# Attention with routed experts on one core: float index tables from GpSimd, three one-row products, and a later first value load

## The chip, the cores and the metric

The kernel runs on one core of a Trainium2 chip. The metric is the device time of one execution in microseconds (us); lower is better. Engines are named as in the profile: PE is TensorE (PEld its weight loads), DVE is VectorE, ACT is ScalarE, POOL is GpSimd, SP is SyncE, which here only issues transfers.

## The reference

Attention over q, k, v of shape (4, 8, 768, 64) with four sink positions and a sliding window of 128, then a two-level mixture of experts over the 3072 tokens of 512 features: a group (of 4) and an expert in it (of 4) are picked by argmax, each expert is a two-layer network (512 to 1024 to 512), and its output is scaled by the product of the two gate probabilities.

```python
scores = scale * np.matmul(q, k.transpose(0, 1, 3, 2))
keep = (pos[None, :] < n_sink) | ((rel >= 0) & (rel < window))
a = softmax(np.where(keep, scores, -1e9))          # rel = query position - key position
x = (a @ v)                                        # as 3072 tokens x 512
g = argmax(x @ w_group); e = argmax(x @ w_expert[g])
out = gate(g) * gate(e) * (relu(x @ w1[g, e]) @ w2[g, e])
```

`n_sink` and `window` are 64-bit inputs, handed over as four 32-bit words.

## The kernel before, in words

One function, `moe_attention`, builds the whole program. The attention goes over 24 tiles of 128 queries (6 tiles in each of 4 batches) in a loop that is written as a pipeline (line 1214): in iteration i the scores of tile i, the transposes and first value products of earlier tiles, the logits of tile i-3 and pieces of the routing are issued. Each engine runs its instructions in the order of the program text (`Pinned`, line 125, keeps that order), so the text of the loop body is the schedule. Behind the loop stand the expert layers, which read 128 weight blocks and scatter their outputs.

A tile's scores are written into two halves of PSUM (four heads each). `maxima(i, g)` (line 770) adds the mask on VectorE and takes the negative maximum, one instruction per head; on tiles that do not begin a batch a predicated copy comes first. `exps(i, g)` (line 782) runs one exponential per head on ScalarE. `trans`, `evac`, `sink_t`, `sink_evac`, `sink_rows` and `sink_pack` transpose the probabilities and bring them to SBUF (ScalarE copies, GpSimd selections); `values` multiplies them with the values; `norm` and `norm_logits` scale the result and add the routing logits on VectorE.

What the change touches is the opening, lines 184 to 312, and three later places:

- Lines 184 to 187: two integer tables by GpSimd iota, `dif` (row minus column) and `coli` (column).
- Lines 268 to 278: VectorE casts both to float (`diff`, `col`), copies the two diagonal 64x64 blocks into `dq`, and makes `isu` (where `dq` is negative) and `rel`.
- Lines 279 to 283: the four words are cast (`nf1`); PE runs `warm(WARM)`, 14 filler matmuls on zeros, then one product of a row of ones with the words, which spreads them to all 128 partitions, then `warm(WARM2)`, six more fillers.
- Lines 286 to 305: the masks of the first tile of a batch (`msk[:, 0]`) and a part of the later ones. The words of each number are put together here: the low word, plus 2**32 where it is negative, plus 2**32 times the high word (`lneg`, `sv`).
- Lines 309 to 314: `other_masks`, called in iteration 0 after the tile's maxima, makes the masks of the other tiles.
- Lines 335 to 344: `tables`, called in iteration 3 after `sink_pack(3)`, makes the constants of the routing, `trib` from `diff` among them.
- Lines 1211 and 1212: the loads of the first sink values (`load_s(0)`, 128 KB) and of tile 0's values (`load_v(0)`, 512 KB), ahead of the loop. All loads but a part of tile 0's keys go through SP's queue. `load_q(i + 2)` and `load_k(i + 2)` stand in the loop; the queries have two buffers, so tile 2's wait for tile 0's scores.

The function `warm(k, dst)` (line 200) issues k filler matmuls. `FILL` gives further fillers in iterations 0 to 2 (8, 10 and 6).

Of the kernel before, what the change touches and what calls it, by code (L numbers as in the profile page):

```python
# [10 lines left out]
F32 = mybir.dt.float32  # L11
F32R = mybir.dt.float32r
BF16 = mybir.dt.bfloat16
I32 = mybir.dt.int32
U32 = mybir.dt.uint32
AF = mybir.ActivationFunctionType
ALU = mybir.AluOpType
# [5 lines left out]
P = 128  # L23
B, H, S, D = 4, 8, 768, 64
# [21 lines left out]
NEG = -1.0e30  # L46
# [55 lines left out]
FIRST = 21  # L102
TAIL = (8, 8)
PW = G + NE
WARM = 14
WARM2 = 6
FILL = [8, 10, 6]


# [38 lines left out]
def moe_attention(tc, kqT, vN, vS, nsw, wgx, wgd, w1, w2, out):  # L148
    nc = Pinned(tc)
    v = nc.vector  # L150
    with ExitStack() as top, ExitStack() as att:
# [5 lines left out]
        gp = fl.enter_context(tc.tile_pool(name="gp", bufs=6, side="left"))  # L157
# [9 lines left out]
        ob = [ps_a.tile([P, DM], F32, name=n) for n in ("lg", "po")]  # L167

        def const(shape, dt, name):
            return cp.tile(shape, dt, name=name)  # L170
# [3 lines left out]
        ni = const([1, 4], I32, "ni")  # L174
        nc.sync.dma_start(ni, nsw)
        colm = const([P, P], F32, "colm")
# [4 lines left out]
        qb = wk.tile([P, NQ, HP, P], F32, name="qb", bufs=1)  # L181
        xx = un[:, 0:NDC * W].rearrange("p (c w) -> p c w", w=W)
        hx = un[:, NDC * W:(NDC + NFC) * W].rearrange("p (f w) -> p f w", w=W)
        dif = gp.tile([P, P], I32, name="xg")
        nc.gpsimd.iota(dif, pattern=[[-1, P]], base=0, channel_multiplier=1)
        coli = gp.tile([P, P], I32, name="xg")
        nc.gpsimd.iota(coli, pattern=[[1, P]], base=0, channel_multiplier=0)
        act = const([P, 1], F32, "act")
        nc.gpsimd.memset(act, 0.0)
        nc.gpsimd.memset(colm[0:1], 1.0)  # L190
        nc.gpsimd.memset(kb[:, :, 0:BW], 0.0)
        vts, env, bat = {}, {}, {}

# [3 lines left out]
        def pair():  # L197
            return ps_p.tile([P, 2, 4 * P], F32, name="tp")

        def warm(k, dst=None):  # L200
            dst = pair()[:, 0, 0:192] if k and dst is None else dst
            for _ in range(k):
                nc.tensor.matmul(dst, wz[:, 0:P], wz, start=True, stop=True)
# [17 lines left out]
        def load_q(i):  # L221
            b, t = divmod(i, NT)
            nc.sync.dma_start(qb[:, i % NQ], kqT[b, t, :, KB:].rearrange("d (h q) -> d h q", h=HP))
# [7 lines left out]
        def room_v(i):  # L231
            vts[i] = wk.tile([P, 2, DM], F32, name="vv", bufs=3)

        def load_v(i):
            room_v(i)
            b, t = divmod(i, NT)
            nc.sync.dma_start(vts[i].rearrange("p f n -> p (f n)"), vN[b, t])

        def load_s(i):
            nc.sync.dma_start(vts[i - 1][SK].rearrange("p f n -> p (f n)"), vS[i // NT])  # L240
# [24 lines left out]

        route_reset(tab)

        diff = const([P, P], F32, "diff")
        v.tensor_copy(diff, dif)
        col = const([P, P], F32, "col")  # L270
        v.tensor_copy(col, coli)
        dq = gp.tile([P, D], F32, name="xg")
        for r in (0, D):
            v.tensor_copy(dq[r:r + D], diff[r:r + D, r:r + D])
        isu = gp.tile([P, D], F32, name="xg")
        v.tensor_scalar(isu, dq, 0.0, None, ALU.is_lt)
        rel = gp.tile([P, D], F32, name="xg")
        v.scalar_tensor_tensor(rel, isu, float(P), dq, ALU.mult, ALU.add)
        nf1 = const([1, 4], F32, "nf1")
        v.tensor_copy(nf1, ni)  # L280
        warm(WARM)
        nc.tensor.matmul(ob[0][:, 0:4], colm[0:1], nf1, start=True, stop=True)
        warm(WARM2)
        msk = const([P, 3, SW], F32, "msk")
        mb, ms, mc = msk[:, :, 0:D], msk[:, :, D:D + 2 * NSK], msk[:, :, D + 2 * NSK:]
        v.tensor_scalar(mb[0:D, 0], dq[0:D], 0.0, NEG, ALU.mult, ALU.add)
        v.tensor_scalar(ms[:, 0, 0:NSK], col[:, 0:NSK], 0.0, NEG, ALU.is_ge, ALU.mult)
        wd = const([P, 1], F32, "wd")
        nf = const([P, 4], F32, "nf")
        v.tensor_copy(nf, ob[0][:, 0:4])  # L290
        lneg = const([P, 2], F32, "lneg")
        v.tensor_scalar(lneg, nf[:, 0::2], 0.0, 4294967296.0, ALU.is_lt, ALU.mult)
        v.tensor_tensor(lneg, lneg, nf[:, 0::2], ALU.add)
        sv = const([P, 2], F32, "sv")
        v.scalar_tensor_tensor(sv, nf[:, 1::2], 4294967296.0, lneg, ALU.mult, ALU.add)
        nsk, win = sv[:, 0:1], sv[:, 1:2]
        v.tensor_scalar(wd, win, -float(D), None, ALU.add)
        snk = gp.tile([P, D], F32, name="xg")
        v.tensor_scalar(mc[:, 2], rel, win, NEG, ALU.is_ge, ALU.mult)
        v.tensor_scalar(snk, col[:, 0:D], nsk, NEG, ALU.is_lt, ALU.mult)  # L300
        v.tensor_scalar(mb[:, 2], dq, wd, NEG, ALU.is_ge, ALU.mult)
        v.scalar_tensor_tensor(mc[:, 0], isu, NEG, mc[:, 2], ALU.mult, ALU.add)
        v.tensor_tensor(mb[D:P, 0], mb[D:P, 2], snk[D:P], ALU.add)
        v.tensor_scalar(ms[:, 0, NSK:], col[:, 0:NSK], nsk, NEG, ALU.is_ge, ALU.mult)
        v.tensor_tensor(mc[0:D, 0], mc[0:D, 0], snk[0:D], ALU.add)
        selu = const([P, D], I32, "selu")
        val = const([P, NI], F32, "val")

        def other_masks():
            v.tensor_scalar(selu, dq, 0.0, None, ALU.is_lt)  # L310
            v.tensor_copy(ms[:, 2], ms[:, 0])
            v.tensor_copy(msk[:, 1], msk[:, 2])
            v.tensor_tensor(snk[0:D], snk[0:D], isu[0:D], ALU.mult)
            v.tensor_tensor(mc[0:D, 1], mc[0:D, 1], snk[0:D], ALU.add)
# [19 lines left out]

        def tables():
            v.tensor_scalar(colm, col, -float(P), None, ALU.add)
            v.tensor_scalar(trib, diff, 0.0, None, ALU.is_lt)
            v.tensor_scalar(rev, col[:, 0:4], -1.0, 4.0, ALU.mult, ALU.add)
            v.tensor_scalar(edge, col[:, 0:MAXT + 1], float(P), None, ALU.mult)
            v.tensor_copy(val, prti)  # L340
            v.tensor_scalar(gen[:, 0:1], win, 1.0, None, ALU.is_lt)
            v.tensor_scalar(gen[:, 1:2], win, float(P), None, ALU.is_gt)
            v.tensor_scalar(gen[:, 2:3], nsk, float(NSK), None, ALU.is_gt)
            v.tensor_reduce(gen[:, 3:4], gen[:, 0:3], AX.X, ALU.max)
# [136 lines left out]
        start = const([P, NE], F32, "start")  # L481
# [177 lines left out]
        xg, cg, later = {}, {}, []  # L659
# [548 lines left out]

        ew = early_work(PARTS[0][0])
        room_v(-1)  # L1210
        load_s(0)
        load_v(0)
        rest = None
        for i in range(NI):
            a, b, c = i - 1, i - 2, i - 3
            mid, far, old = a >= 0, b >= 0, c >= 0
            state["clk"] += 3.0
            scores(i, 0)
            scores(i, 1)
            if i + DEPTH < NI:  # L1220
                load_q(i + DEPTH)
            if mid:
                env["tp"] = pair()
                trans(a)
                evac(a, 0)
                evac(a, 1)
            warm(FILL[i] if i < len(FILL) else 0, ob[0][:, 224:416])
            if far:
                values(b, 0)
                load_s(b + 1)  # L1230
            if i + DEPTH < NI:
                load_k(i + DEPTH)
            if i == 0:
                load_v(1)
            if old:
                logits(c)
            if mid:
                sink_t(a)
            if old:
                natural(c)  # L1240
            maxima(i, 0)
            exps(i, 0)
            maxima(i, 1)
            if i == NI - 1:
                sink_evac(a)
            if old:
                norm(c)
            routing(1, ("pe",))
            exps(i, 1, (0, 1))
            if mid and i < NI - 1:  # L1250
                sink_evac(a)
            exps(i, 1, (2, 3))
            if mid:
                sink_rows(a)
            if i < NI - 1:
                sink_pack(i)
            if old:
                norm_logits(c)
            if i == 0:
                late_consts()  # L1260
            if i == 3:
                tables()
            state["clk"] += 3.0
            if far:
                values(b, 1)
                load_v(i)
                out_evac(b)
            if rest:
                rest()
                rest = None  # L1270
            put_gates(3)
            if later and not gates:
                gather(*later.pop(0))
            routing(UNITS.get(i, REND), (None, "rd"))
            if i and i % 2 == 0:
                sums(i - 1)
            rest = half.pop()() if half else wjob() if i < NI - 1 else None
            if i in HOOK:
                prefetch(min(RAW, len(raws) + 1))
# [372 lines left out]
```

## Time and profile before

| what | value |
|---|---|
| median of 3 runs | 489.07 us (487.38 to 489.42) |
| time of the profiled execution | 484.39 us |
| span of the profiled execution | 482.7 us |
| PE busy | 465.3 us (96%) |
| VectorE busy | 374.7 us (78%) |
| ScalarE busy | 330.2 us (68%) |
| GpSimd busy | 168.4 us (35%) |
| chain that ended last, by engine | PE 67%, DVE 17%, ACT 7%, issue 4%, POOL 3%, DMA 1% |

Times in the views are microseconds from the start of the span. A busy time counts instructions in flight; in a chain of waits each piece is followed by the work that it released. In a timeline a number in brackets is the idle time of the engine before the row, and behind the arrow what ended it.

### The profile page before, as it was taken

Reading aid. Unit: us, or ns where it says so; the run is one execution under the profiler, and the core shown is the slowest. Engines: PE = TensorE matmul, PEld = TensorE weight load, DVE = VectorE, ACT = ScalarE, POOL = GpSimd, SP = SyncE. Lnnn points to the kernel's source line nnn. Section 1 sums busy time; section 2 is a strip of 40 time slices with the busy share of each in tenths; the row PEclk is TensorE's granted clock in tenths of the full one; section 3 lists DMA queues with packets and bytes.
Section 4 is the critical chain, followed back from the end, with each engine's and each line's share of the span. In section 5 each row is a group of like instructions: output and inputs, shape, how many; then the busy total and the mean of one; then the engine's idle time right before and its main releaser. Section 6 shows DMA issues by size and latency. Waiting matters only on the chain.

```text
span 482.7 us, 14712 instructions
## 1 busy us (share of the span) xinstructions
PE 465.3 (96%) x5429; PEld 390.0 (81%) x5429; DVE 374.7 (78%) x1181; ACT 330.2 (68%) x858; POOL 168.4 (35%) x267
## 2 busy tenths in 40 slices
PE   7999999999989999999999999999999999999994
PEld 6788878888779888887989789569876977977974
DVE  7576888899989989987714876488687997999750
ACT  5999989899893445766615765278446786788741
POOL 3674765664662122221203124033302713103102
PEclk9999999999999999999999999999999999999998
DMA  8698878989978937934952358596949983999300
GB/s 260 177 286 277 275 250 245 272 258 318 289 233 274 336 103 245 311 135 150 377 217 85 110 176 299 197 330 267 311 169 372 411 314 111 362 405 337 108 22 30
DMA packets 58836, 117.09 MB, mean 243 GB/s; under 512 B 8574, under 2 KB 20990, under 8 KB 58754
## 3 DMA queue, kind: packets, MB, share of 16 engines
q1 hardware_dynamic: 54162, 102.65, 62.5%
q0 software_dynamic: 4320, 13.26, 7.8%
q8 instruction: 45, 0.74, 0.6%
q14 instruction: 37, 0.30, 0.2%
q10 hardware_dynamic: 272, 0.15, 0.1%
HBM read 103.25 MB, written 13.03 MB: 241 GB/s over the span
## 4 chain that ended last, share of the span: by engine, by line
PE 67%; DVE 17%; ACT 7%; issue 4%; POOL 3%; DMA 1%; POOLq 0%; DVEq 0%; SPq 0%; ACTq 0%
PE ph L118 30%; PE po L118 28%; PE tp L118 5%; ACT pt L118 3%; DVE sm L118 3%; DVE wlo L118 3%; PE ps L118 3%; DVE xt L118 2%; POOL pu L118 2%; ACT whi L118 1%; PE lg L118 1%; DVE ps L118 1%; ACT pa L118 1%; DVE lt L118 1%; DVE un L118 1%
## 5 line engine op out<-in xcount | busy, mean ns | idle before, releaser
L118 DVE TENSOR_TENSOR wlo<-rw,whi 128x1024 fp32r<-128x1024 f32 x112 | 135.0, 1223 | 24.9 <-ACT whi L118 23.5
L118 PE MATMUL ph<-un,whi 128*128 128x256 f32 (+9 forms) x576 | 128.0, 312 | 0.3
L118 PE MATMUL po<-whi,un 128*128 128x512 f32 (+5 forms) x384 | 127.8, 396 | 0.0
L118 ACT CAST whi<-rw 128x1024 fp32r<-128x1024 f32 (+1 forms) x115 | 115.6, 1025 | 10.5 <-DMA rw<-in_w 5.6
L118 POOL DMA_INDIRECT out<-ot,sidx x32 | 43.2, 1351 | 227.7 <-ACT ot L118 129.3
L118 PE MATMUL ph<-un,wlo 128*128 128x256 f32 (+10 forms) x416 | 99.1, 263 | 0.0
L118 PEld LDWEIGHTS ph<-un,whi 128*128 128x128 f32 x576 | 93.7, 189 | 2.2 <-DVE un L118 0.8
L118 PEld LDWEIGHTS po<-whi,un 128*128 128x128 f32 (+4 forms) x384 | 70.4, 185 | 25.1 <-issue 6.7
L118 ACT ACTIVATE pt<-sm,st 128x136 f32<-128x136 f32 x192 | 76.1, 402 | 7.4 <-DVE st L118 5.3
L118 PE MATMUL po<-wlo,un 128*128 128x512 f32 (+6 forms) x200 | 77.5, 389 | 0.0
L118 PEld LDWEIGHTS ph<-un,wlo 128*128 128x128 f32 x416 | 76.7, 189 | 0.6
L118 DVE CUSTOM_DVE_ANT_0 sm<-ps,msk 128x136 f32<-128x136 f32 x192 | 45.8, 296 | 7.3 <-PE ps L118 1.1
L118 PEld LDWEIGHTS po<-wlo,un 128*128 128x128 f32 (+5 forms) x200 | 36.0, 180 | 7.6
L118 POOL DMA_INDIRECT xg<-xd,gidx x30 | 33.1, 1104 | 24.2 <-DMA rw<-in_w 11.6
L118 PE MATMUL ps<-kb,qb 64*64 64x208 f32 (+1 forms) x768 | 38.4, 333 | 2.0 <-DVE st L118 1.4
L118 DVE TENSOR_TENSOR hc<-ph,hc 128x160 f32<-128x160 f32 (+6 forms) x64 | 21.3, 338 | 21.6 <-ACT hc L118 21.4
L118 POOL COPY pu<-spT 32x512 f32<-32x512 f32 x46 | 28.6, 649 | 26.3 <-ACT spT L118 25.4
L118 ACT ACTIVATION_READ_ACCUMULATOR pt<-sm,st 128x1 f32 x192 | 36.8, 192 | 0.0
L118 ACT ACTIVATE ot<-po,cg 128x512 f32<-128x512 f32 (+6 forms) x25 | 17.0, 681 | 28.1 <-PE po L118 28.1
L118 PEld LDWEIGHTS ps<-kb,qb 64*64 64x64 f32 x768 | 26.5, 132 | 7.3 <-DVE st L118 2.1
L118 POOL TENSOR_SCALAR_AFFINE_SELECT pu<-pa 64x512 f32<-64x512 f32 x40 | 26.4, 660 | 15.7 <-ACT pa L118 15.7
L118 ACT COPY hc<-ph 128x160 f32<-128x160 f32 (+6 forms) x64 | 19.4, 304 | 17.8 <-PE ph L118 17.0
(204 smaller groups left out, 717.6 us busy)
## 6 DMA issues: line engine op xcount, KB each, us to landing
rw<-in_w SPq DMA_DIRECT2D x128, 512.0 KB, 5.9
vv<-in_vN SPq DMA_DIRECT2D x24, 512.0 KB, 5.2
kb<-in_kqT SPq DMA_DIRECT2D x23, 288.0 KB, 3.9
qb<-in_kqT SPq DMA_DIRECT2D x24, 256.0 KB, 4.6
xd<-xt SPq DMA_DIRECT2D x24, 256.0 KB, 3.7
vv<-in_vS SPq DMA_DIRECT2D x24, 128.0 KB, 3.5
out<-ot,sidx POOLq DMA_INDIRECT x32, 4.9
xg<-xd,gidx POOLq DMA_INDIRECT x30, 4.9
```

The source lines that it names most:

```text
L118: r = f(*a, **k)
```

## The change

GpSimd writes the index tables as float: the two diagonal blocks straight into `dq`, and `col`; the casts and copies on VectorE are gone, and so is the full table `diff` in the opening. `tables()` makes `diff` when it needs it, by an iota of its own. The scalars' sign is taken from the cast words on one partition, and three products (low words by 1, sign flags by 2**32, high words by 2**32) add up in PSUM, with one filler behind each; VectorE copies the sum once. The mask of tile 0 is made from a table `relx` in which the upper part is already far away, and from `far`, which is `dq` plus 64. The table and the mask of the later tiles (`rel`, `mc[:, 2]`) move into `other_masks()`. The fillers go from 14 and 6 to 11 and 1. The two first value loads move into iteration 0, behind `load_k(2)`.

```diff
--- before.py
+++ after.py
@@ -102,8 +102,8 @@
 FIRST = 21
 TAIL = (8, 8)
 PW = G + NE
-WARM = 14
-WARM2 = 6
+WARM = 11
+WARM2 = 1
 FILL = [8, 10, 6]
 
 
@@ -181,13 +181,21 @@
         qb = wk.tile([P, NQ, HP, P], F32, name="qb", bufs=1)
         xx = un[:, 0:NDC * W].rearrange("p (c w) -> p c w", w=W)
         hx = un[:, NDC * W:(NDC + NFC) * W].rearrange("p (f w) -> p f w", w=W)
-        dif = gp.tile([P, P], I32, name="xg")
-        nc.gpsimd.iota(dif, pattern=[[-1, P]], base=0, channel_multiplier=1)
-        coli = gp.tile([P, P], I32, name="xg")
-        nc.gpsimd.iota(coli, pattern=[[1, P]], base=0, channel_multiplier=0)
+        mk = gp.tile([P, 6, D], F32, name="xg")
+        dq, far, isu, rel, relx, snk = (mk[:, k] for k in range(6))
+        col = const([P, P], F32, "col")
+
+        def count(out, **k):
+            nc.gpsimd.iota(out, base=0, allow_small_or_imprecise_dtypes=True, **k)
+
+        for r in (0, D):
+            count(dq[r:r + D], pattern=[[-1, D]], channel_multiplier=1)
+        count(col, pattern=[[1, P]], channel_multiplier=0)
         act = const([P, 1], F32, "act")
         nc.gpsimd.memset(act, 0.0)
         nc.gpsimd.memset(colm[0:1], 1.0)
+        two32 = gp.tile([1, P], F32, name="xg")
+        nc.gpsimd.memset(two32, 4294967296.0)
         nc.gpsimd.memset(kb[:, :, 0:BW], 0.0)
         vts, env, bat = {}, {}, {}
 
@@ -265,48 +273,35 @@
 
         route_reset(tab)
 
-        diff = const([P, P], F32, "diff")
-        v.tensor_copy(diff, dif)
-        col = const([P, P], F32, "col")
-        v.tensor_copy(col, coli)
-        dq = gp.tile([P, D], F32, name="xg")
-        for r in (0, D):
-            v.tensor_copy(dq[r:r + D], diff[r:r + D, r:r + D])
-        isu = gp.tile([P, D], F32, name="xg")
         v.tensor_scalar(isu, dq, 0.0, None, ALU.is_lt)
-        rel = gp.tile([P, D], F32, name="xg")
-        v.scalar_tensor_tensor(rel, isu, float(P), dq, ALU.mult, ALU.add)
-        nf1 = const([1, 4], F32, "nf1")
-        v.tensor_copy(nf1, ni)
+        v.scalar_tensor_tensor(relx, isu, -NEG, dq, ALU.mult, ALU.add)
+        v.tensor_scalar(far, dq, float(D), None, ALU.add)
+        nf1 = const([1, 6], F32, "nf1")
+        v.tensor_copy(nf1[:, 0:4], ni)
+        v.tensor_scalar(nf1[:, 4:6], nf1[:, 0:4:2], 0.0, None, ALU.is_lt)
         warm(WARM)
-        nc.tensor.matmul(ob[0][:, 0:4], colm[0:1], nf1, start=True, stop=True)
-        warm(WARM2)
+        for k, (w, x) in enumerate(((colm[0:1], nf1[:, 0:4:2]), (two32, nf1[:, 4:6]), (two32, nf1[:, 1:4:2]))):
+            nc.tensor.matmul(ob[0][:, 0:2], w, x, start=k == 0, stop=k == 2)
+            warm(WARM2)
         msk = const([P, 3, SW], F32, "msk")
         mb, ms, mc = msk[:, :, 0:D], msk[:, :, D:D + 2 * NSK], msk[:, :, D + 2 * NSK:]
         v.tensor_scalar(mb[0:D, 0], dq[0:D], 0.0, NEG, ALU.mult, ALU.add)
         v.tensor_scalar(ms[:, 0, 0:NSK], col[:, 0:NSK], 0.0, NEG, ALU.is_ge, ALU.mult)
-        wd = const([P, 1], F32, "wd")
-        nf = const([P, 4], F32, "nf")
-        v.tensor_copy(nf, ob[0][:, 0:4])
-        lneg = const([P, 2], F32, "lneg")
-        v.tensor_scalar(lneg, nf[:, 0::2], 0.0, 4294967296.0, ALU.is_lt, ALU.mult)
-        v.tensor_tensor(lneg, lneg, nf[:, 0::2], ALU.add)
         sv = const([P, 2], F32, "sv")
-        v.scalar_tensor_tensor(sv, nf[:, 1::2], 4294967296.0, lneg, ALU.mult, ALU.add)
+        v.tensor_copy(sv, ob[0][:, 0:2])
         nsk, win = sv[:, 0:1], sv[:, 1:2]
-        v.tensor_scalar(wd, win, -float(D), None, ALU.add)
-        snk = gp.tile([P, D], F32, name="xg")
-        v.tensor_scalar(mc[:, 2], rel, win, NEG, ALU.is_ge, ALU.mult)
         v.tensor_scalar(snk, col[:, 0:D], nsk, NEG, ALU.is_lt, ALU.mult)
-        v.tensor_scalar(mb[:, 2], dq, wd, NEG, ALU.is_ge, ALU.mult)
-        v.scalar_tensor_tensor(mc[:, 0], isu, NEG, mc[:, 2], ALU.mult, ALU.add)
-        v.tensor_tensor(mb[D:P, 0], mb[D:P, 2], snk[D:P], ALU.add)
+        v.tensor_scalar(mc[:, 0], relx, win, NEG, ALU.is_ge, ALU.mult)
+        v.tensor_scalar(mb[:, 2], far, win, NEG, ALU.is_ge, ALU.mult)
         v.tensor_scalar(ms[:, 0, NSK:], col[:, 0:NSK], nsk, NEG, ALU.is_ge, ALU.mult)
         v.tensor_tensor(mc[0:D, 0], mc[0:D, 0], snk[0:D], ALU.add)
+        v.tensor_tensor(mb[D:P, 0], mb[D:P, 2], snk[D:P], ALU.add)
         selu = const([P, D], I32, "selu")
         val = const([P, NI], F32, "val")
 
         def other_masks():
+            v.scalar_tensor_tensor(rel, isu, float(P), dq, ALU.mult, ALU.add)
+            v.tensor_scalar(mc[:, 2], rel, win, NEG, ALU.is_ge, ALU.mult)
             v.tensor_scalar(selu, dq, 0.0, None, ALU.is_lt)
             v.tensor_copy(ms[:, 2], ms[:, 0])
             v.tensor_copy(msk[:, 1], msk[:, 2])
@@ -334,6 +329,8 @@
 
         def tables():
             v.tensor_scalar(colm, col, -float(P), None, ALU.add)
+            diff = gp.tile([P, P], F32, name="xg")
+            count(diff, pattern=[[-1, P]], channel_multiplier=1)
             v.tensor_scalar(trib, diff, 0.0, None, ALU.is_lt)
             v.tensor_scalar(rev, col[:, 0:4], -1.0, 4.0, ALU.mult, ALU.add)
             v.tensor_scalar(edge, col[:, 0:MAXT + 1], float(P), None, ALU.mult)
@@ -1208,8 +1205,6 @@
 
         ew = early_work(PARTS[0][0])
         room_v(-1)
-        load_s(0)
-        load_v(0)
         rest = None
         for i in range(NI):
             a, b, c = i - 1, i - 2, i - 3
@@ -1231,6 +1226,8 @@
             if i + DEPTH < NI:
                 load_k(i + DEPTH)
             if i == 0:
+                load_s(0)
+                load_v(0)
                 load_v(1)
             if old:
                 logits(c)
```

## Rows read from the trace of the kernel before

**Rows 1.** Chain of waits in the opening: start us, us, what.
```profile
1.13 2.42 PE tp L118 x14
```
**Rows 2.** Timeline, ScalarE: first exponentials of tiles 0 and 4 (start us, us, instruction, idle before).
```profile
6.79 0.41 ACT L118 ACTIVATE pt<-sm,st 128x136 f32<-128x136 f32 x1 [4.01 <-DVE st L118]
...
27.06 0.42 ACT L118 ACTIVATE pt<-sm,st 128x136 f32<-128x136 f32 x1
```
**Rows 3.** Busy time in two stretches: us, PE, PEld, DVE, ACT, POOL, PEclk, DMA share, GB/s.
```profile
24.00:48.00 24.00, 23.45 (x622) 20.29 (x616) 17.86 (x100) 22.94 (x88) 14.54 (x28) 1.00 0.89 281
...
200.00:300.00 100.00, 100.00 (x627) 86.83 (x626) 66.65 (x142) 59.47 (x115) 22.19 (x21) 1.00 0.57 203
```
**Rows 4.** Timeline, PE, from the product to the fillers behind tile 0's scores.
```profile
3.48 0.59 PE L118 MATMUL lg<-nf,colm 1*128 1x4 f32 x2
4.00 0.87 PE L118 MATMUL tp<-wz 128*128 128x192 bf16 x6
4.81 1.16 PE L118 MATMUL ps<-kb,qb 64*64 64x136 f32 x32
5.90 0.83 PE L118 MATMUL lg<-wz 128*128 128x192 bf16 x8
```
**Rows 5.** Timeline, VectorE, from its first instruction to tile 0's first maximum.
```profile
1.38 0.84 DVE L118 CAST diff<-xg 128x128 f32<-128x128 int32 x1 [1.38 <-POOL xg L118]
...
3.17 0.15 DVE L118 CAST nf<-ni 1x4 f32<-1x4 int32 x1
...
4.11 0.16 DVE L118 COPY nf<-lg 128x4 f32<-128x4 f32 x1 [0.62 <-PE lg L118]
4.30 0.17 DVE L118 TENSOR_SCALAR lneg<-nf 128x2 f32<-128x2 f32 x1
...
5.13 0.25 DVE L118 TENSOR_SCALAR xg<-col,sv 128x64 f32<-128x64 f32 x1
5.29 0.25 DVE L118 TENSOR_SCALAR msk<-xg,wd 128x64 f32<-128x64 f32 x1
...
5.70 0.22 DVE L118 TENSOR_TENSOR msk<-msk,xg 64x64 f32<-64x64 f32 x1
5.94 0.23 DVE L118 TENSOR_SCALAR msk<-col,sv 128x4 f32<-128x4 f32 x1
6.08 0.21 DVE L118 TENSOR_TENSOR msk<-msk,xg 64x64 f32<-64x64 f32 x1
6.45 0.30 DVE L118 CUSTOM_DVE_ANT_0 sm<-ps,msk 128x136 f32<-128x136 f32 x1 [0.16 <-DVE msk L118]
```
**Rows 6.** Timeline, GpSimd: the two iotas.
```profile
1.12 0.42 POOL L118 IOTA xg<- 128x128 int32 x2
```
**Rows 7.** Transfers between 1.7 and 1.8, SP's queue: packets, MB, share.
```profile
q1 hardware_dynamic: 2, 0.00, 1.0%
```
**Rows 8.** Timeline, SP's queue and PE: a value load, tile 1's scores, tile 0's values.
```profile
6.88 0.50 SPq L118 DMA_DIRECT2D vv<-in_vN  x1
...
8.08 1.64 PE L118 MATMUL ps<-kb,qb 64*64 64x208 f32 x32 [1.35 <-DVE st L118]
...
15.88 1.15 PE L118 MATMUL po<-pa,vv 128*64 128x64 f32 x32
```
**Rows 9.** Page, transfers by kind: count, KB each, us from issue to landing.
```profile
vv<-in_vN SPq DMA_DIRECT2D x24, 512.0 KB, 5.2
```
**Rows 10.** Timeline, GpSimd: sink copies of tiles 0 and 3.
```profile
10.09 0.21 POOL L118 COPY sp<-pt 128x32 f32<-128x32 f32 x1 [6.95 <-ACT pt L118]
...
10.24 0.19 POOL L118 MEMSET sacc<- 128x16 f32 x3
...
25.55 0.21 POOL L118 COPY sp<-pt 128x32 f32<-128x32 f32 x1
```
**Rows 11.** Timeline, VectorE: the routing table and tile 4's first maximum.
```profile
23.91 0.21 DVE L118 TENSOR_SCALAR trib<-diff 128x128 bf16<-128x128 f32 x1
...
25.35 0.30 DVE L118 CUSTOM_DVE_ANT_0 sm<-ps,msk 128x136 f32<-128x136 f32 x1
```

## The prediction

> **What bounds the kernel now.** I read the page first (96% of the span PE is busy), then the chain of waits from its start, the stretches, and the timeline of each engine where the diff touches it. The reader is to see two things.
>
> First, the chain starts with fillers: 14 matmuls from 1.13 for 2.42 us, 0.17 each [rows 1]. Behind them lie the product that spreads the two scalars over 128 partitions and VectorE's masks, up to the first mask-and-maximum instruction of tile 0 at 6.45. ScalarE's first exponential follows at 6.79, 0.34 later [rows 2]. Second, from there on nothing is loose: in the stretch 24 to 48 ScalarE is busy 22.94 and PE 23.45 of 24 us, and between 200 and 300 PE is busy 100.00 of 100 [rows 3]. So a shift of the first exponential travels to the end, and a stall of ScalarE in the first 48 us does so too, unless one of the few gaps takes it back.
>
> **Own time.** The profiled execution took 484.39 us, its span 482.7; the 1.69 around it I leave as it is. The median of the runs shown is 489.07, 4.68 above. Sums are made against 484.39 and the difference is carried to the median. About 0.5% (2.4 us) is what a measurement of this kernel can tell from no change.
>
> **The change part by part.**
>
> *Casts and tables.* Before, VectorE starts with two int32 casts at 1.38 and reaches the cast of the scalars at 3.17; the product follows 0.31 later at 3.48 [rows 4, 5]. Now GpSimd writes float tables: two iotas took 0.42 together [rows 6], VectorE began 0.26 after the first, so with a second before it it begins near 1.6. Five instructions follow there, at most 0.24 apart (5.70 to 5.94, [rows 5]), the scalars' cast as fourth: 1.6 + 3 x 0.24 = 2.32, readable for PE 0.31 later at 2.63. The scalars themselves are there: the queue's first two small packets fall before 1.8 [rows 7]. The 11 fillers last until 1.13 + 11 x 0.17 = 3.03, so they hide all of this; float iotas of twice the length (0.42 more) would put it at 3.05, still level. This edit costs and gives nothing by itself; it lets three fillers go.
>
> *Three products.* One product holds PE from 3.48 to the next filler at 4.00, 0.52, and its result reaches VectorE 0.11 after that [rows 4, 5]. Three with two fillers between, all in a row: 3.03 + 3 x 0.52 + 2 x 0.17 + 0.11 = 5.04. If fillers stream while the next weights load, 4.70. At the higher of PE's two levels a product would be half, and 3.03 + 3 x 0.26 + 0.11 = 3.92. The levels show in the fillers: 0.17 each before, 0.83/8 = 0.10 from 5.90 [rows 1, 4]. The row nearest to the new products is the old one, at the low level, so I take 4.80, against 4.11 before: 0.69 given away.
>
> *Shorter masks.* From the copy of the product (4.11) to the first maximum (6.45) VectorE takes 2.34. Gone are the two steps for negative words, the combination, the window less 64, and one table with its mask of the later tiles. Left behind the copy: 0.19 to the next dependent instruction, three one-input instructions at 0.16, 0.14 behind the small one, 0.24 for a two-input one, 0.37 from the last to the maximum [rows 5]: 0.19 + 0.48 + 0.14 + 0.24 + 0.37 = 1.42, or 0.92 less. The first maximum so comes at 4.80 + 1.42 = 6.22, **0.23 earlier**. Ends: 5.04 + 1.42 = 6.46, no gain; and 3.92 + 1.42 = 5.34, which the scores forbid in part: they begin at 4.81 and the first of two halves of 1.16 is done near 5.4 [rows 4], so 5.5 and a gain of 0.95.
>
> *Loads moved.* PE began tile 1's scores at 8.08 after 1.35 idle [rows 8], though VectorE, with four heads at 0.24 or less each from 6.45, had read the first half of tile 0 by 7.4. What came last is then tile 1's keys, and the two value loads (512 and 128 KB) were issued right behind them. They now go behind tile 2's keys, past two issues of the SP queue, to where 6.88 stands [rows 8]. A value load lands 5.2 us after its issue [rows 9], two in a row by about 13; tile 0's values are first multiplied at 15.88 [rows 8]. What is queued behind them, tile 1's values and the gate weights, moves back by two issues of 0.5 and is needed later still. Free, and it is the condition for the gain above: if tile 1's scores stay at 8.08, tile 0's transposes, which run behind them, start no earlier, and the 0.23 stops there.
>
> Here a page speaks against the change. The Trainium skill, "DMA: Bandwidth & Descriptors", Queues, rings and completion order, says that each DMA engine takes the descriptors of one ring in order. By it loads issued behind the keys could not hold them up, and the move would give nothing; no row here settles it, and it is a rival below.
>
> *Two masks moved.* The table and the mask of the later tiles (0.24 + 0.16 = 0.40) now run between tile 0's and tile 1's maxima. Cover: ScalarE is then inside eight exponentials of about 0.4 from 6.79 [rows 2]. Zero; 0.40 if that cover were gone.
>
> *The iota moved into the routing tables.* This one costs. GpSimd keeps program order: at tile 0 its memsets stood behind the sink copy, which waited 6.95 us for ScalarE, and came 0.15 after it [rows 10]. The routing tables come behind tile 3's sink copy, which ran at 25.55 [rows 10]. So the iota starts at 25.55 + 0.15 = 25.70 and VectorE's table can start 0.26 later (as 1.12 to 1.38), at 25.96; before it ran at 23.91 [rows 11]. VectorE stands 2.05 us, and behind that instruction on its queue are tile 4's maxima: 25.35 [rows 11] becomes 27.40. ScalarE can start tile 4's exponentials 0.34 after, at 27.74; before it started at 27.06 [rows 2]. The first 1.37 are hidden and **0.68 is lost**, where ScalarE has no gap. Ends: with an iota that costs VectorE nothing beyond its start, 25.70, so 0.42; with one 0.26 longer, 0.94.
>
> *Small memsets on GpSimd* lie in the 6.95 us in which it waited anyway [rows 10].
>
> **Sum:** 484.39 - 0.23 + 0.68 = 484.84, that is +0.45, or 489.5 at the median.
>
> **The rivals.**
>
> 1. *The keys come no earlier.* For it: the loads that are moved were issued behind them. Against: PE's 1.35 idle with its input free [rows 8]. The opening gains nothing and the table's wait stays: 484.39 + 0.68 = 485.07, 489.75.
>
> 2. *The table's wait is taken back.* If ScalarE regains the 0.68 in a gap behind (its share of 24 to 48 leaves 1.06 us, [rows 3]), the opening alone counts: 484.39 - 0.23 = 484.16, 488.8. Against: the gaps are waits for PE, which is just as full.
>
> 3. *PE stays at the low level (the other side).* The granted clock in the stretches reads 1.00 [rows 3], yet fillers of 0.17 and of 0.10 show the 1.2 and 2.4 GHz levels. Before, the engine ran 20 fillers nearly without a break before the scores [rows 1, 4]; now 14, with products between them. If the rise comes only after tile 1's scores, these pay 1.64 more, tile 0's 1.16, eight fillers 8 x 0.07 = 0.56 [rows 4, 8]; less the 1.35 that PE was idle, 2.0. With +0.45 and at least 0.1 for the transposes behind, +2.55: 486.9, 491.6, slower by just over 0.5%. It decides where the rise falls: ahead of tile 1's scores it costs little. The Trainium skill, "TensorE: Matmul & The Clock Gate", What's actually happening, calls the low level the default that activity releases, which is this mechanism. Against: PE has work without a long break from 3.0 on in either kernel.
>
> 4. *The opening gives all it can* (0.95) and the wait takes its least (0.42): -0.53, 483.86, 488.5.
>
> **How the numbers follow.** The forecast has 0.50, the first rival 0.20, the second 0.14, the third 0.06, the fourth 0.07; 0.03 is left for a gain of over 0.5% that I see no source of. Only the third case is beyond 0.5% on the slow side. So faster 0.03, same 0.91, slower 0.06. The likeliest time is 489.5. The cases other than the third run from 488.5 to 490.0 (no gain, wait 0.94); the runs shown reach 1.69 below and 0.35 above their median, which a new median can share in part. I give 487.0 to 490.6, leaving out the third case.
>
> **What would show it.** In the profile after: the first product near 3.0 and the copy of its sum near 4.8; the first exponential near 6.6; tile 1's scores at 7.5 or before; GpSimd's iota right behind a sink copy, and VectorE idle about 2 us for it ahead of tile 4's maxima, with ScalarE idle some 0.7 there. A first exponential after 6.8 breaks the second and third steps; tile 1's scores still held by the keys makes it the first rival; no ScalarE gap at tile 4 the second; scores of tile 1 lasting 3 us instead of 1.64 the third. A change of over 2 us in any stage after 48 would make the whole reading wrong.

## The result, and the profile after

The changed kernel is slower: 491.11 us median of 18 runs (488.67 to 496.91) against 487.45 of the kernel before over as many, ratio 1.0065, 95% interval 1.0047 to 1.0083. One of the 18, the 496.91, fell into a slower state of the chip, and the ratio leaves it out. The forecast was 489.5 and no change. The 1.6 us between 489.5 and 491.11 understate the miss, because the base moved the other way: the three runs shown at first had a median of 489.07, the eighteen 487.45. By the ratio the change costs 0.65%, about 3.2 us, where the forecast had 0.45.

| what | after |
|---|---|
| time of the profiled execution | 491.54 us |
| span | 489.8 us |
| PE busy | 471.2 us (96%) |
| VectorE busy | 374.7 us (76%) |
| ScalarE busy | 329.8 us (67%) |
| chain, by engine | PE 73%, DVE 9%, ACT 7%, POOL 4%, issue 4%, DMA 1% |

The chain of waits of the changed kernel in its opening (start us, us, what):

```profile
1.13 1.94 PE tp L118 x11
...
5.57 2.02 PE ps L118 x32
7.59 1.39 PE lg L118 x8
8.98 2.03 PE ps L118 x32
11.02 0.66 PE tp L118 x16
...
11.70 1.07 ACT pa L118 x2
```

The same stretch in the timeline of PE:

```profile
3.17 0.55 PE L118 MATMUL lg<-nf,colm 1*128 1x2 f32 x2
...
3.93 0.58 PE L118 MATMUL lg<-nf,xg 1*128 1x2 f32 x2
...
4.71 0.58 PE L118 MATMUL lg<-nf,xg 1*128 1x2 f32 x2
...
5.50 2.09 PE L118 MATMUL ps<-kb,qb 64*64 64x136 f32 x32
7.52 1.46 PE L118 MATMUL lg<-wz 128*128 128x192 bf16 x8
8.91 2.10 PE L118 MATMUL ps<-kb,qb 64*64 64x208 f32 x32
```

ScalarE's first copy of transposes in the kernel before, and its first exponentials of tiles 0 and 4 in the changed kernel:

```profile
10.40 1.07 ACT L118 COPY pa<-tp 128x512 f32<-128x512 f32 x2 [0.37 <-PE tp L118]
```

```profile
7.12 0.41 ACT L118 ACTIVATE pt<-sm,st 128x136 f32<-128x136 f32 x1 [4.34 <-DVE st L118]
...
28.99 0.41 ACT L118 ACTIVATE pt<-sm,st 128x136 f32<-128x136 f32 x1 [0.53 <-DVE st L118]
```

Before, the chain went from the product into VectorE's masks and maxima. Now it stays on PE from the first filler to the copy: fillers, three products, tile 0's scores in 2.09 (1.16 in [rows 4]), eight fillers in 1.46 (0.83), tile 1's scores in 2.10 (1.64 in [rows 8]), and only then the transposes of tile 0 that ScalarE copies at 11.70. In the kernel before that copy stood at 10.40. The first exponential came at 7.12 instead of 6.79 [rows 2].

VectorE in the changed kernel, its timeline, beside [rows 5]:

```profile
1.58 0.92 DVE L118 TENSOR_SCALAR xg<-xg 128x64 f32<-128x64 f32 x1 [1.58 <-POOL xg L118]
...
5.33 0.16 DVE L118 COPY sv<-lg 128x2 f32<-128x2 f32 x1 [1.67 <-PE lg L118]
5.53 0.25 DVE L118 TENSOR_SCALAR xg<-col,sv 128x64 f32<-128x64 f32 x1
...
6.78 0.30 DVE L118 CUSTOM_DVE_ANT_0 sm<-ps,msk 128x136 f32<-128x136 f32 x1 [0.16 <-PE ps L118]
...
27.27 0.23 DVE L118 TENSOR_SCALAR trib<-xg 128x128 bf16<-128x128 f32 x1 [1.98 <-POOL xg L118]
```

The sum of the products is copied at 5.33 instead of 4.11, the first maximum comes at 6.78 instead of 6.45, and the routing table waits 1.98 us for GpSimd's iota (the instruction that writes the counted table).

**A measure for all runs.** I follow one instruction that each tile has once: VectorE's scaling of the finished tile (`xt<-tp,rc`). Its start in a kernel less its start in the first profile of the kernel before is called the lag. The kernel before, tiles 0, 1 and 3:

```profile
22.88 0.69 DVE L118 TENSOR_TENSOR xt<-tp,rc 128x512 f32<-128x512 f32 x1 [0.65 <-ACT pt L118]
...
28.14 0.69 DVE L118 TENSOR_TENSOR xt<-tp,rc 128x512 f32<-128x512 f32 x1 [0.37 <-PE tp L118]
...
38.83 0.69 DVE L118 TENSOR_TENSOR xt<-tp,rc 128x512 f32<-128x512 f32 x1 [1.64 <-ACT pt L118]
```

The changed kernel:

```profile
24.16 0.69 DVE L118 TENSOR_TENSOR xt<-tp,rc 128x512 f32<-128x512 f32 x1 [0.64 <-ACT pt L118]
...
30.92 0.69 DVE L118 TENSOR_TENSOR xt<-tp,rc 128x512 f32<-128x512 f32 x1
...
40.84 0.69 DVE L118 TENSOR_TENSOR xt<-tp,rc 128x512 f32<-128x512 f32 x1 [1.49 <-ACT pt L118]
```

So the lag is 1.28 from the opening, 2.78 behind the routing tables, and 2.01 at tile 3, where VectorE has taken back half of its wait. It stays between 1.6 and 2.0 to tile 16. Then a step of 3.2 follows at tile 17. Past the tiles the lag is taken in the same way from ScalarE's outputs of the expert layers (`ot<-po,cg`): one step of 1.2 lies between 183 and 208, and smaller ones lead to 6.9 at the end. The experiments had to say which of these belong to the change.

### The profile page after: what moved, and what is told of

Read it like the earlier page. It is cut to its first block, busy times and chain, and to the rows that moved or that the text cites. A ratio compares the mean times of both kernels' runs of the same rounds, so it can differ in the third digit from the quotient of the medians.

```text
span 489.8 us, 14703 instructions
## 1 busy us (share of the span) xinstructions
PE 471.2 (96%) x5427; PEld 393.1 (80%) x5427; DVE 374.7 (76%) x1176; ACT 329.8 (67%) x858; POOL 168.5 (34%) x270
## 4 chain that ended last, share of the span: by engine, by line
PE 73%; DVE 9%; ACT 7%; POOL 4%; issue 4%; DMA 1%; SPq 0%; POOLq 0%; DVEq 0%; ACTq 0%
PE ph L118 32%; PE po L118 31%; PE tp L118 6%; PE ps L118 3%; ACT pt L118 3%; DVE sm L118 2%; POOL pu L118 2%; PE lg L118 2%; ACT pa L118 2%; ACT whi L118 1%; DMA rw<-in_w 1%; DVE xt L118 1%; DVE wlo L118 1%; POOL pa L118 1%; DVE ps L118 1%
## 5 line engine op out<-in xcount | busy, mean ns | idle before, releaser
L118 PE MATMUL ps<-kb,qb 64*64 64x208 f32 (+1 forms) x768 | 40.9, 347 | 2.5 <-issue 2.5
L118 POOL DMA_INDIRECT xg<-xd,gidx x30 | 33.1, 1103 | 24.3 <-DVE sidx L118 11.7
L118 PEld LDWEIGHTS ps<-kb,qb 64*64 64x64 f32 x768 | 27.7, 139 | 8.7 <-issue 3.9
L118 ACT ACTIVATE un<-ph 128x256 fp32r<-128x256 f32 (+1 forms) x40 | 15.2, 383 | 25.7 <-PE ph L118 23.3
```

The source lines that it names most:

```text
L118: r = f(*a, **k)
```

## The experiments

Each of the timed ones ran 12 times beside the kernel before on the same chip. At first I held two theories. A: the opening leaves PE at its low level and the iota holds VectorE. B: the loss is later, where the step at tile 17 stands.

**The changed kernel again**, without an edit.

> The changed kernel as it is, for its second profile. Theory A (the opening leaves PE at its low level, and the iota in the routing tables holds VectorE): tile 0's scores last 2.0 us or more again, the first transposes' copy on ScalarE comes 1.0 us or more later than in the kernel before, VectorE waits about 2 us ahead of tile 4's maxima, and at tile 9 the lag is 1.5 to 2.3. Theory B (most of the loss comes later, where PE stood 1.85 us in the scores at 118.8 and then ran at half its clock): the lag of about 3 us at that place comes again, and the ratio to the kernel before stays near 1.0065. If A alone holds, that step is missing or elsewhere and the ratio lies near 1.004.

Measured: 489.92 us, ratio 1.0059 (1.0032 to 1.0087). The lag is 1.35, 2.84 and 2.07 at tiles 0, 1 and 3 and 1.79 at tile 17: the step of 3.2 is not there, the opening's 1.3 and the table's wait are. B falls as the main cause. A's 1.004 lies inside the interval, but not at its middle.

**The routing table's iota in the opening.**

```diff
         route_reset(tab)
+        diff = const([P, P], F32, "diff")
+        count(diff, pattern=[[-1, P]], channel_multiplier=1)
...
             v.tensor_scalar(colm, col, -float(P), None, ALU.add)
-            diff = gp.tile([P, P], F32, name="xg")
-            count(diff, pattern=[[-1, P]], channel_multiplier=1)
```

> The table for the routing is written by GpSimd in the opening instead of in iteration 3. Theory A: VectorE's idle time of 1.98 us ahead of tile 4's maxima is gone, the lag behind the kernel before is the same at tile 1's norm as at tile 0's (about 1.3 us), 0.5 to 0.8 us better than the changed kernel, ratio near 1.005. Rival (the wait is hidden and taken back): the lag from tile 3 on is the changed kernel's 2.0, the ratio 1.0065.

Measured: 489.05 us, ratio 1.0030 (1.0001 to 1.0060). Its scalings of tiles 0, 1 and 3, from the timeline:

```profile
24.94 0.69 DVE L118 TENSOR_TENSOR xt<-tp,rc 128x512 f32<-128x512 f32 x1 [0.64 <-ACT pt L118]
...
30.20 0.69 DVE L118 TENSOR_TENSOR xt<-tp,rc 128x512 f32<-128x512 f32 x1 [0.37 <-PE tp L118]
...
40.88 0.69 DVE L118 TENSOR_TENSOR xt<-tp,rc 128x512 f32<-128x512 f32 x1 [1.63 <-ACT pt L118]
```

The lag is 2.06, 2.06 and 2.05: flat, where the changed kernel rose by 1.50 and kept 0.73. The number that was expected for tile 3, about 1.3, did not come; 2.05 is the rival's 2.0. But it stands there from tile 0 on, because the opening itself lost more this time, 2.06, and the table adds nothing to it. So the iota's place costs 0.73 that stays, and the rival (taken back) falls. The other profiles agree: with the late iota the lag grows from tile 0 to tile 3 by 0.71 to 0.74 (by 1.00 in one of five), with the early one by 0.02 at most (three). Why the opening lost more shows on PE:

```profile
8.92 2.87 PE L118 MATMUL ps<-kb,qb 64*64 64x208 f32 x32
```

All of tile 1's scores ran at the low level; it rose later still. The end result hides this; the lag shows both.

**One product instead of three**, the rest of the change kept.

```diff
-WARM = 11
-WARM2 = 1
+WARM = 14
+WARM2 = 6
...
-        for k, (w, x) in enumerate(((colm[0:1], nf1[:, 0:4:2]), (two32, nf1[:, 4:6]), (two32, nf1[:, 1:4:2]))):
-            nc.tensor.matmul(ob[0][:, 0:2], w, x, start=k == 0, stop=k == 2)
-            warm(WARM2)
+        nc.tensor.matmul(ob[0][:, 0:4], colm[0:1], nf1, start=True, stop=True)
+        warm(WARM2)
...
+        v.tensor_scalar(lneg, nf[:, 0::2], 0.0, 4294967296.0, ALU.is_lt, ALU.mult)
+        v.tensor_tensor(lneg, lneg, nf[:, 0::2], ALU.add)
...
+        v.scalar_tensor_tensor(sv, nf[:, 1::2], 4294967296.0, lneg, ALU.mult, ALU.add)
```

> The changed kernel with the one product, its 14 and 6 fillers and the combination on VectorE put back; float tables, moved masks, moved loads and the late iota stay. Theory A: PE reaches its high level before tile 0's scores (these 1.2 us, tile 1's 1.64), the first exponential comes at 6.3 to 6.6, ahead of 6.79 of the kernel before, and only the table's wait of 0.5 to 0.7 us is left: ratio 1.000 to 1.002. Theory B: the lag comes back at the later places, ratio 1.004 or more.

Measured: 487.67 us, ratio 1.0010 (0.9978 to 1.0041). The first exponential came at 6.72. PE, timeline:

```profile
3.57 0.55 PE L118 MATMUL lg<-nf,colm 1*128 1x4 f32 x2
4.06 1.14 PE L118 MATMUL tp<-wz 128*128 128x192 bf16 x6
5.13 2.09 PE L118 MATMUL ps<-kb,qb 64*64 64x136 f32 x32
7.15 0.91 PE L118 MATMUL lg<-wz 128*128 128x192 bf16 x8
8.00 1.64 PE L118 MATMUL ps<-kb,qb 64*64 64x208 f32 x32
```

Here A's expectation missed in two points: tile 0's scores ran at the low level (2.09) although 20 fillers stood ahead of them, the level rising only near 7.3, and the first exponential came behind the 6.3 to 6.6 that were expected. Yet the lag at tile 0 is -0.08. It becomes 1.41 and then 0.65 through the table's wait alone. So a low level over tile 0's scores loses nothing against the kernel before, and what the opening loses by is the three products, or the thinner fillers that came with them; this run undoes both.

**The loads alone**, in the kernel before.

```diff
         room_v(-1)
-        load_s(0)
-        load_v(0)
...
             if i == 0:
+                load_s(0)
+                load_v(0)
                 load_v(1)
```

> The kernel before with the first value loads moved behind tile 2's keys and nothing else. If the value loads held up tile 1's keys, tile 1's scores start near 7.5 instead of 8.08. If the ring's order kept the keys ahead anyway, they start at 8.0 to 8.1 as before. Either way the first exponentials stay at 6.8 and the time within 0.3% of the kernel before.

Measured: 486.69 us, ratio 0.9982 (0.9958 to 1.0007). PE, timeline:

```profile
7.47 1.81 PE L118 MATMUL ps<-kb,qb 64*64 64x208 f32 x32 [0.47 <-DVE st L118]
```

Tile 1's scores start at 7.47, behind the four maxima of their half, and not at 8.08 [rows 8]: the value loads did hold up the keys, and the move takes 0.61 off that wait. The lag is 0.00 at tile 0, since ScalarE's exponentials end last there: its first copy of transposes still comes at 10.40.

**Twenty fillers around the three products**, in the changed kernel.

```diff
-WARM = 11
-WARM2 = 1
+WARM = 14
+WARM2 = 6
...
             nc.tensor.matmul(ob[0][:, 0:2], w, x, start=k == 0, stop=k == 2)
-            warm(WARM2)
+        warm(WARM2)
```

> The changed kernel with its three products back to back behind 14 fillers and six fillers behind them. Theory A (products thinned by single fillers leave PE at its low level until about 10): the level rises before tile 1's scores, by 8 at the latest; these last 1.64 to 1.8, the lag at tile 0's norm falls from 1.3 to 0.3 to 0.7 although the first maximum comes as late as 6.5 to 7.2; with the table's 0.72 on top 1.0 to 1.4 from tile 3 on, ratio 1.002 to 1.004. Rival (the level has nothing to do with the fillers and the late products are the whole loss): the lag at tile 0's norm stays at 1.3 or more.

Measured: 490.84 us, ratio 1.0072 (1.0040 to 1.0103), lag 1.49 at tile 0, 2.24 at tile 3. PE, timeline:

```profile
3.48 0.58 PE L118 MATMUL lg<-nf,colm 1*128 1x2 f32 x2
3.93 0.99 PE L118 MATMUL lg<-nf,xg 1*128 1x2 f32 x4
4.85 1.14 PE L118 MATMUL tp<-wz 128*128 128x192 bf16 x6
5.92 2.09 PE L118 MATMUL ps<-kb,qb 64*64 64x136 f32 x32
7.95 1.46 PE L118 MATMUL lg<-wz 128*128 128x192 bf16 x8
9.34 1.84 PE L118 MATMUL ps<-kb,qb 64*64 64x208 f32 x32
```

A's account of the fillers falls and the rival's 1.3 or more comes: with all 20 back the eight behind tile 0's scores still take 1.46, so the level rises no earlier than about 9.3. Back to back the three products take 1.37 (3.48 to 4.85), 0.46 each, against 0.77 from one to the next in the changed kernel: the single fillers between them cost 0.3 each. With the same 20 fillers, one product lagged by -0.08 and three by 1.49; so the three products lose the opening, with either set of fillers.

**Eleven and one fillers in the kernel before**, nothing else (`WARM = 11`, `WARM2 = 1`).

> The kernel before with 11 and 1 fillers instead of 14 and 6, nothing else. Theory A: the level rises later than the 4.3 to 7.2 of the profiles with 14 and 6 fillers, behind tile 1's scores or in them (9 to 11), tile 0's norm lags by 0.5 to 1.5 though every mask comes at its old time; ratio 1.001 to 1.003. Rival (the products, not the missing fillers, keep the level low): tile 0's scores start earlier, near 4.2, the level rises by 7.5, lag 0.1 or less, ratio 0.999 to 1.001.

Measured: 487.36 us, ratio 0.9994 (0.9960 to 1.0028), lag 0.26. PE, timeline:

```profile
4.23 2.09 PE L118 MATMUL ps<-kb,qb 64*64 64x136 f32 x32
6.25 1.46 PE L118 MATMUL lg<-wz 128*128 128x192 bf16 x8
7.78 2.17 PE L118 MATMUL ps<-kb,qb 64*64 64x208 f32 x32
```

The level is as low as in the changed kernel and rises nearly as late, inside tile 1's scores, and little is lost: these scores start 0.58 earlier than in the kernel before [rows 4]. Both readings that I had written down missed their numbers and were half right: thinner fillers go with a late rise, and a low level by itself costs little.

That left theory C: PE stood idle for 1.35 us ahead of tile 1's scores in the kernel before [rows 8]; late scores fit into that, and a low level nearly does, but not both.

**The kernel before with eleven fillers behind its product** (`WARM2 = 11`): late scores, high level.

> The kernel before with eleven fillers instead of six behind its product: tile 0's scores start late (5.3 to 5.9 against 4.8 to 5.1), PE without a gap. Theory C: a late start alone fits into the cover, lag at tile 0's norm 0.0 to 0.4, ratio 0.999 to 1.002. Rival (what counts is only when tile 0's scores start): lag 0.5 or more with a high level by 7.

Measured: 486.67 us, ratio 1.0031 (1.0001 to 1.0061), lag 0.11 at tiles 0 to 4. PE, timeline:

```profile
5.48 1.16 PE L118 MATMUL ps<-kb,qb 64*64 64x136 f32 x32
6.57 0.83 PE L118 MATMUL lg<-wz 128*128 128x192 bf16 x8
8.20 1.64 PE L118 MATMUL ps<-kb,qb 64*64 64x208 f32 x32 [0.79 <-DVE st L118]
```

Tile 0's scores start at 5.48, as late as in the changed kernel (5.50), but take 1.16, and the lag is 0.11 instead of 1.28. For the profile this is C: PE still stood 0.79 idle, so the late scores took nothing. The ratio is above what I expected; its interval nearly reaches 1.000, and the opening has no place for 0.3%, so the time neither confirms nor refutes it.

**The changed kernel without the eight fillers behind tile 0's scores** (`FILL = [0, 10, 6]`), alone and with the early iota.

> The changed kernel without the eight fillers behind tile 0's scores. Theory C (late scores and a low level share one cover, the 1.35 us in which PE stood ahead of tile 1's scores; each fits, both together overflow it): without the 1.46 us of fillers on that path tile 1's scores start near 7.8 to 8.3 instead of 8.9, ScalarE's first copy of transposes comes at 10.8 to 11.3 instead of 11.7, tile 0's norm lags 0.4 to 0.8 instead of 1.3, from tile 3 on 1.1 to 1.5. Rival (those fillers are what raises the level): tile 1's scores last 2.9 or more, the lag stays 1.3 or grows. Ratio 1.002 to 1.005 by C.

> The same with the routing table's iota in the opening too: the two repairs of the changed kernel that leave its three products. By theory C the lag is that of tile 0's norm in the run without the fillers, 0.4 to 0.8, and stays so to tile 8; ratio 1.000 to 1.003. By the rival 1.3 or more, ratio 1.003 or more.

Measured: 487.16 us, ratio 1.0028 (1.0004 to 1.0053), and 487.51 us, 1.0027 (0.9996 to 1.0058). In the first, timelines of PE and ScalarE:

```profile
7.80 2.15 PE L118 MATMUL ps<-kb,qb 64*64 64x208 f32 x32 [0.20 <-DVE st L118]
...
10.74 1.07 ACT L118 COPY pa<-tp 128x512 f32<-128x512 f32 x2 [0.37 <-PE tp L118]
...
19.33 0.93 PE L118 MATMUL ps<-kb,qb 64*64 64x208 f32 x16 [0.67 <-DMA kb<-in_kqT]
```

The copy of the transposes comes 0.96 earlier than in the changed kernel, as C wants, and the lag at tile 0 is 0.81, at the end of what C allows. Only 0.34 of that is the copy (10.74 against 10.40), and it is the delay of the first exponential; the rest appears with a new wait, 0.67 us for tile 3's keys. At tile 3 the lag is 1.81, where I had expected 1.1 to 1.5. The second:

```profile
7.80 3.05 PE L118 MATMUL ps<-kb,qb 64*64 64x208 f32 x32 [0.20 <-DVE st L118]
```

Here tile 1's scores lasted 3.05, and the lag is 1.22 from tile 0 to tile 7, flat as in the other runs with the early iota. That is outside C's 0.4 to 0.8 and near the rival's 1.3. The path is C's in both: the copy follows the work on PE, 0.96 earlier in the first and hardly earlier (11.64) in the second, where the scores took 0.9 longer. Whether those fillers also raise the level is not shown: without them it rose near 8.9 in the first profile and behind 10.3 in the second. That the two together come out no better than the first is within their intervals.

**The parts that should be free together**: float tables, moved masks and loads, one product with 14 and 6 fillers, the iota early.

> Float tables from GpSimd, moved masks and moved loads, but one product with 14 and 6 fillers and the routing table's iota in the opening: the parts of the change that cost nothing by theory A. Expected: the first exponential at 6.3 to 6.75, VectorE without a wait at the routing tables, the lag from tile 0 on between -0.3 and 0.0, ratio 0.998 to 1.001. If the float tables themselves cost (GpSimd's writes beside VectorE), the first exponential is at 6.8 or later and the lag positive.

Measured: 487.89 us, ratio 0.9997 (0.9965 to 1.0029). The first exponential comes at 6.48, VectorE has no wait at the routing tables, the lag is -0.27 at tile 0 and -0.24 at tile 3. This is the only kernel that is ahead of the old one throughout its opening, by a quarter of a microsecond that the time cannot show.

**The kernel before again**, for a second profile.

> The kernel before again, for a second profile. If the later steps of the lag (near 117 to 122 where PE stood in the scores, near 190 to 205, and past 400) come and go from execution to execution, some of them show here without any edit, and tile 0's norm lags by less than 0.1. If they are due to the edits, all landmarks agree within 0.3 us up to the end.

Measured: 487.29 us. PE:

```profile
5.07 1.79 PE L118 MATMUL ps<-kb,qb 64*64 64x136 f32 x32
...
8.44 1.64 PE L118 MATMUL ps<-kb,qb 64*64 64x208 f32 x32 [0.81 <-DVE st L118]
```

PE's level rose inside tile 0's scores, which took 1.79. That did no harm, for PE then stood idle for 0.81 again; but tile 1's scores started at 8.44, 0.36 later than in the first profile, though VectorE's maxima came at the same times. What is left for PE to wait for is tile 1's loads, as in the first profile. So the lag is 0.38 at tile 0 without any edit: single tenths of the lag are noise. It goes on to 1.17 at tile 5, 1.69 at 170, 2.88 from 208 on and 3.39 past 405. So the steps near 200 and past 400 come without any edit; the first profile, 484.39, was one of the quickest executions. In all profiles only the part of the lag before 44 us can be read against the edits. In that part lag and time agree: the lag at tile 3, as a share of 487.45, lies inside the interval of the ratio in each of the ten runs that were timed, wide as the intervals are. Only for the first eighteen it falls a little short, 0.41% against 0.47 to 0.83.

**The step at tile 17** in the changed kernel, PE's timeline, and the stretch with it:

```profile
118.80 2.06 PE L118 MATMUL ps<-kb,qb 64*64 64x208 f32 x20 [1.85 <-issue]
```

```profile
118.00:120.00 2.00, 1.20 (x18) 1.20 (x19) 0.62 (x2) 1.03 (x2) 0.87 (x2) 0.78 1.06 369
120.00:122.00 2.00, 2.00 (x26) 1.29 (x22) 1.77 (x14) 0.05 (x1) 0.00 (x0) 0.50 1.01 277
```

PE stops inside a tile's scores for something that the profile does not show, and the granted clock (the third column from the right) falls to 0.50 behind the stop. Such a stop stands in 4 of the 13 profiles (the changed kernel, the loads alone and the two without eight fillers), all with the moved loads; five others with the moved loads lack it, and the loads alone measured 0.9982. In one of the four the clock stayed at 1.00 over the stop and the 4 us behind it. Whether the loads make the stop likelier stays open.

## Why the prediction was wrong, step by step

- **Casts and tables.** The first product came at 3.17, not 3.03. VectorE began at 1.58 (I had 1.6), but its first instruction took 0.92 beside GpSimd's writes, where a like one takes 0.25 at 5.53. Small, and on the path, because the fillers end before it. The Trainium skill, "GPSIMD Engine Reference", Specifications, says that GpSimd shares its SBUF interfaces with VectorE, and that it contends there with some VectorE instructions. The trace agrees in part, as do the 0.84 of the old cast and the 0.21 of a table of the same size [rows 5, 11]; but in two of the eight profiles with float tables the same instruction took 0.33 beside the same iota, and what decides that is not shown.
- **Three products: failed.** I took 4.80 for the copy, with 5.04 at worst; it was 5.33. The term was 0.52 + 0.17 for a product and its filler; it measured 0.77. Back to back a product takes 0.46, so the two changes between product and filler add about 0.14 to the two of them (0.46 + 0.17). With the first product 0.14 late, the 5.04 becomes 5.34.
- **Shorter masks: right.** 5.33 to 6.78 is 1.45, against 1.42.
- **The path behind it: failed, and this is the main step.** I priced the opening by its first exponential alone and wrote that the first maximum comes 0.23 earlier. The way that set the end ran on PE. In the rows: start of tile 0's scores 5.50 less 4.81 = 0.69; their length 2.09 less 1.16 = 0.93; eight fillers 1.46 less 0.83 = 0.63; tile 1's scores 2.10 less 1.64 = 0.46; less the 1.35 that PE stood idle there: 1.36, and the copy of the transposes came 11.70 less 10.40 = 1.30 later. Late scores alone (0.11, with PE idle all the same) and a low level alone (0.26) cost little each. The first exponential was late as well, by 0.33, and that alone would have set the copy at 10.74, where it stands without the eight fillers; the other 0.96 is PE's.
- **Rival 3 was this, with 0.06.** Its place and mechanism were right. Its price of 2.0 lies inside what the runs with three products and eight fillers show, 1.28 to 2.06, in part by luck: it had 1.64 for tile 1's scores, which paid 0.46, and nothing for their later start. I had set against it that PE has work without a long break from 3.0 on; it had, and the level still rose only near 9.9. What misled me was the single profile: the rise at about 4.5 there is the earliest of all. Read from the spacing of single matmuls, it fell between 4.5 and 7.3 with 20 or more fillers and one product (six profiles), and between 8.9 and 11.7 with three products or 12 fillers (seven). The Trainium skill, "TensorE: Matmul & The Clock Gate", What's actually happening, calls low the default state. The traces agree: in all 13 the first fillers take 0.17 each; no run here shows what exactly brings the rise.
- **Loads moved: right in kind.** The keys do come earlier when nothing is issued behind them: tile 1's scores start at 7.47, against 8.08. The conclusion I had drawn against it from the ring's order (the Trainium skill, "DMA: Bandwidth & Descriptors", Queues, rings and completion order) is decided by the measurement. That page's order is one of taking descriptors, not of finishing them, so it did not carry the conclusion.
- **The iota in the tables: right.** VectorE's wait 1.98 (I had 2.05), what stays of it 0.73 (0.68); with the iota early it is gone. ScalarE waits 0.53 at tile 4's first exponential, which comes 1.93 late, 0.65 more than the opening's 1.28.
- **Two masks moved: free, as I had it.** VectorE runs them from 8.54 to 9.05 and still waits 0.51 for tile 1's scores.
- **Sum.** Opening +1.28 to +2.06 where I had -0.23, table +0.73 where I had +0.68: 2.0 to 2.8 us, 0.41 to 0.57% of 487.45, against 0.65% measured (0.47 to 0.83). The step that failed is the opening's: its path, and the price of the three products on it. What lies between is inside the interval; no run assigns it.

## What to carry to other kernels

An idle stretch on an engine is one budget for all delays of an edit together: here 1.35 us would have covered late scores or most of a slow PE, not both, so add up every delay on the same engine before calling one of them covered. A helper instruction that moves behind an engine's waiting work passes that wait on to whoever reads its result; place constants ahead of the loop. Before pricing a start by one profile, look at a second one: the point where PE reaches its high level moved from 4.5 to 6.3 between two executions of the same kernel, and lay at 7.3 in a like opening.

## What the runs showed of the hardware that I had not expected

A chain of one-row products costs far more between fillers than alone: 0.77 from one to the next with a filler in between, 0.46 without. The granted clock of the profile's stretches, two microseconds each, read 1.00 from 0 to 12 us in the changed kernel while PE ran at half its speed for most of that time (fillers 0.17 apart, scores 2.09 instead of 1.16), so in an opening the level has to be read from durations. And two loads issued behind the keys in the same queue delayed them: without them tile 1's scores started at 7.47, with them at 8.08, and at 8.20 and 8.44 in the two other profiles where PE stood idle ahead of them.
